# The causal mask of the first three units: from a VectorE product to a ScalarE copy and a GpSimd selection

## The chip, the cores and the metric

The kernel runs on one core of a Trainium2 chip. The core has five engines that work at the same time, each through its own queue in order: TensorE (matrix products and transposes, PE in the profile; PEld is its weight load), VectorE (DVE), ScalarE (ACT), GpSimd (POOL) and SyncE (SP), which here only issues transfers from the chip's main memory. TensorE writes its results to PSUM, a small memory of its own; the other tiles are in SBUF. The metric is the device time of one execution in microseconds, taken as the median of several runs.

## The reference

Two blocks follow one another. The first is a gated linear attention over 4 batches, 8 heads, 768 steps and a head size of 48. For each batch and head a 48x48 state decays by a gate and takes in one key and value at each step:

```python
f = 1.0 / (1.0 + np.exp(-f_logit))
for t in range(S):
    state = f[:, :, t, :, None] * state + np.einsum('bhd,bhe->bhde', k[:, :, t], v[:, :, t])
    y[:, :, t] = np.einsum('bhd,bhde->bhe', q[:, :, t], state)
```

The second mixes its output x, laid out as (4, 768, 384), along the sequence through a product of rank 32, and then along the channels through a hidden layer of 1536:

```python
u = x + h.transpose(0, 2, 1)          # h = x^T @ U @ V
out = u + np.maximum(u @ w_ch1, 0.0) @ w_ch2
```

All of it is float32.

## The kernel before

The sequence is cut into 12 chunks of 64 steps. Inside a chunk, each query meets the keys of its own and the earlier steps by a matrix product; between chunks the 48x48 states are carried by a scan. A **unit** is one batch and one pair of heads, so there are 16 units, `n = 0..15`, four to a batch (`HP = 4`). The two heads of a pair lie on two halves of the 128 partitions.

The work of a unit has a front and a rear. The front (`prepare`, line 643) has the pieces `gates` (transposes of the gates on TensorE, line 660, then a sigmoid on ScalarE, lines 681 and 682), `keep` (a backward scan of gate products on VectorE, L694, a small ScalarE copy `least`, L699, and three small VectorE operations, L701 to L704), `keys` (transposes of k, L660, and their product with that scan, L672), `read_back` (a forward scan, L712) and `queries` (transposes of q, L660, and their product with the forward scan, L672).

The rear (`attend`, line 770) has `kept` (transposes of k, L809, two ScalarE copies, `whole` L813 and `kb` L815), `states` (the chunk sums `ds`, L825, and a copy, L831), `scan` (the scan over chunks on VectorE, L846), `scores` (48 small products `sc`, L788, and the masked copy `A`, L795), `read` (products of the queries with the states, `y` L863, and a ScalarE copy of two columns, `seen` L870) and `inner` (products of `A` with the values added into the same `y`, L881, and the copy of `y` into `x`, L887).

A tile `A` is 128 x (2 heads, 6 blocks, 64 columns): 768 numbers for each partition. Partitions 0 to 63 hold one of a pair of chunks, 64 to 127 the other. In each 64x64 block the row is the key's step and the column the query's step, so an element counts where the column isn't smaller than the row. `causal` (lines 574 to 579) is a 128x64 tile of ones, zeroed elsewhere by two GpSimd selections of 64x64, and the mask is a product of the scores in PSUM with it.

The first batch has no channel mixing to stand beside it. Its four units run in a loop of their own (line 967), and the order of the pieces there is written out by hand for TensorE, VectorE and ScalarE; SyncE's and GpSimd's queues are ordered by the planner. In step `n` of that loop come:

```python
pieces = front(n, "keep", "keys") + rear(n - 1, "scan", "scores")
pieces += [lambda: busy(3)] + rear(n, "kept") + front(n, "read_back", "queries")
if n + 1 < HP:
    pieces += front(n + 1, "gates") + rear(n - 1, "read", "inner") + rear(n, "states")
```

So the scores of units 0, 1 and 2 are made in steps 1, 2 and 3 of this loop. The scores of unit 3 come just after it, and those of units 4 to 15 beside the mixing of the batch before. `busy(3)` is three matmuls into a tile that nobody reads (L962, tile `idle`).

The tiles in PSUM of the kind `ps_big` turn through three buffers: k's transposes, `sc`, `kept`'s transposes, q's transposes, the next unit's gates, `y` and `ds` take one after another. `A` has two buffers in SBUF. The rank-32 weights are put together from 64-bit words by ScalarE, VectorE and then a GpSimd sum, L95, beginning with `U` right after the loop.

A second path, `general_path`, stands behind a test on the gates and isn't run with these inputs.

Of the kernel before, what the change touches and what calls it, by code (L numbers as in the profile page):

```python
# [15 lines left out]
ALU = mybir.AluOpType  # L16
# [456 lines left out]
def factored_path(ctx, tc, q, k, v, f_logit, moe_U, moe_V, moe_w_ch1, moe_w_ch2, out, ok):  # L473
# [4 lines left out]
    nc = tc.nc  # L478
    B, H, S, D = q.shape
    P = nc.NUM_PARTITIONS  # L480
    C = P // 2
    NCH = S // C

    NBL = S // P
    HP = H // 2
# [90 lines left out]
    for s in range(2):  # L576
        half = causal[s * C : (s + 1) * C, :]
        nc.gpsimd.affine_select(out=half, in_=half, compare_op=ALU.is_ge, fill=0.0, base=0,
                                pattern=[[1, C]], channel_multiplier=-1)
# [190 lines left out]
    def attend(n):  # L770

        b, hp = divmod(n, HP)
        T = units[n]
# [4 lines left out]
        part = [slice(s * C, (s + 1) * C) for s in range(2)]  # L778

        def scores():  # L780


            T["A"] = two.tile([P, 2, NBL, C], F32, name="A")
            sc = ps_big.tile([P, 2, 512], F32, name="sc", tag="big")
            for c in range(NBL):
                for par in range(2):
                    for s in range(2):
                        nc.tensor.matmul(  # L788
                            sc[part[s ^ par], par, c * C : (c + 1) * C],
                            lhsT=T["k"][rows[par], chunk[2 * c + s]],  # L790
                            rhs=T["q"][rows[par], chunk[2 * c + s]],
                            start=True, stop=True,
                        )
            with tc.high_priority(offset=AHEAD):
                nc.vector.tensor_tensor(  # L795
                    T["A"],
                    sc[:, :, 0 : NBL * C].rearrange("p h (c i) -> p h c i", i=C),
                    causal.unsqueeze(1).unsqueeze(1).broadcast_to((P, 2, NBL, C)),
                    ALU.mult,
                )  # L800
# [71 lines left out]
        def inner():  # L872
# [18 lines left out]
            del units[n], v_tiles[n]  # L891

        return [kept, states, scan, scores, read, inner]

    ahead, here = {}, {}
# [59 lines left out]
    with tc.manual_schedule(engines={nc.vector.engine, nc.scalar.engine}):  # L955
# [62 lines left out]
        n = len(m.seconds) // (NBL // 2)  # L1018
# [386 lines left out]
```

## Time and profile before

| what | value |
| --- | --- |
| median of 5 runs | 489.61 us (489.17, 489.47, 489.61, 490.28, 494.36) |
| the profiled execution, its own time | 488.14 us |
| its span, from the first to the last instruction | 486.4 us |
| granted TensorE clock, mean | 0.995 |

Busy times of the first stretches (us):

| stretch | PE | DVE | ACT | POOL |
| --- | --- | --- | --- | --- |
| 0 to 14 | 10.68 | 7.17 | 4.65 | 4.68 |
| 14 to 24 | 8.83 | 9.50 | 4.04 | 0 |
| 24 to 33 | 8.74 | 8.20 | 4.01 | 0 |
| 33 to 40 | 6.86 | 5.80 | 2.86 | 0 |
| 40 to 47 | 4.63 | 5.77 | 3.54 | 1.84 |

A group in the profile is read as: line, engine, operation, the tile written, the tiles read, the shapes (partitions x elements), the count, then the busy time and the mean of one in nanoseconds, the idle time of the engine just before, and what ended it. In a timeline a row begins with the start and the duration in microseconds. The chain of waits goes back from the last instruction to what released each. The mask as a group, and GpSimd's selections in order of time:

```profile
L795 DVE TENSOR_TENSOR A<-sc,causal 128x768 f32<-128x768 f32 x16 | 15.2, 947 | 9.9 <-PE sc L788 9.9
```

```profile
2.21 0.23 POOL L578 TENSOR_SCALAR_AFFINE_SELECT causal<-causal 64x64 f32<-64x64 f32 x1
2.40 0.29 POOL masks.py:199 TENSOR_SCALAR_AFFINE_SELECT ident<-ident 128x128 f32<-128x128 f32 x1
2.76 0.24 POOL L578 TENSOR_SCALAR_AFFINE_SELECT causal<-causal 64x64 f32<-64x64 f32 x1
```

### The profile page before, as it was taken

How to read it: one execution, taken by the hardware profiler on the slowest of the kernel's cores; microseconds unless marked ns; L12 is line 12 of the kernel's file. 1: busy time of each engine (PE TensorE's matmuls, PEld its weight loads, DVE VectorE, ACT ScalarE, POOL GpSimd, SP SyncE). 2: the span in 40 equal slices, each digit the busy share in tenths (PEclk: the TensorE clock that was granted, in tenths of full speed). 3: DMA queues.
4: the chain of work that ended last, by engine and by line, in shares of the span. 5: the costliest groups of instructions: out<-in, count | busy, mean ns of one | idle time of the engine just before them, and what ended most of it. 6: DMA issues, size and time to landing. Idle time of an engine off the chain costs nothing.

```text
span 486.4 us, 12734 instructions
## 1 busy us (share of the span) xinstructions
PE 470.3 (97%) x5541; PEld 401.3 (82%) x5541; DVE 355.4 (73%) x563; ACT 163.3 (34%) x309; POOL 37.7 (8%) x49
## 2 busy tenths in 40 slices
PE   7997999999999999999999999999999999999995
PEld 4775788886566568899899888899979999999995
DVE  5888689777999757656857548797896886958642
ACT  2445566563334313424231403433231312112200
POOL 3002245453000000000000000000000000000000
PEclk9999899999999999999999999999999999999999
DMA  9979975666777512333536100100000000000001
GB/s 144 160 156 168 251 205 151 156 137 82 109 118 116 105 36 32 56 44 67 77 50 97 24 18 18 27 3 20 19 1 1 33 2 18 16 1 34 1 33 38
DMA packets 158679, 34.34 MB, mean 71 GB/s; under 512 B 149206, under 2 KB 157078, under 8 KB 158614
## 3 DMA queue, kind: packets, MB, share of 16 engines
q1 hardware_dynamic: 158614, 33.44, 37.3%
q8 instruction: 45, 0.74, 0.6%
q14 instruction: 20, 0.16, 0.1%
HBM read 28.70 MB, written 4.72 MB: 69 GB/s over the span
## 4 chain that ended last, share of the span: by engine, by line
PE 79%; DVE 9%; DMA 3%; issue 3%; SPq 2%; ACT 2%; DVEq 0%; ACTq 0%
PE pw L312 26%; PE pz L258 23%; PE pp L410 11%; PE y L863 2%; PE pt L660 2%; PE sc L788 2%; PE ds L825 2%; PE y L881 2%; DMA late<-in_f_logit_dram 2%; PE put L246 2%; PE po L283 2%; PE idle L962 2%; DVE late L712 1%; PE pt L809 1%; SPq L554 1%
## 5 line engine op out<-in xcount | busy, mean ns | idle before, releaser
L258 PE MATMUL pz<-uT,w 128*128 128x256 f32 x504 | 115.7, 383 | 0.0
L258 PEld LDWEIGHTS pz<-uT,w 128*128 128x128 f32 x504 | 93.4, 190 | 12.8
L312 PE MATMUL pw<-w,z_all 128*128 128x192 f32 x216 | 37.7, 329 | 0.0
L312 PE MATMUL pw<-zw,w_raw 128*128 128x192 f32 x216 | 37.4, 327 | 0.0
L312 PEld LDWEIGHTS pw<-zw,w_raw 128*128 128x128 f32 x216 | 35.2, 190 | 0.8 <-issue 0.6
L312 PEld LDWEIGHTS pw<-w,z_all 128*128 128x128 f32 x216 | 35.0, 190 | 0.7
L95 POOL TENSOR_TENSOR w<-w_y,w_r 128x384 int32<-128x384 int32 x24 | 31.5, 1313 | 41.7 <-DVE w_y L94 34.7
L694 DVE TENSOR_TENSOR_SCAN late<-fz,late 128x768 f32<-128x768 f32 x16 | 28.1, 1755 | 8.7 <-ACT fz L681 4.3
L268 ACT ACTIVATE z_all<-pz 128x512 f32<-128x512 f32 x33 | 19.7, 596 | 40.0 <-PE pz L258 39.9
L410 PE MATMUL pp<-v_nat,late 128*128 128x128 f32 x224 | 28.8, 275 | 0.0
L712 DVE TENSOR_TENSOR_SCAN late<-fz,other 128x768 f32<-128x768 f32 x16 | 27.9, 1745 | 0.1
L410 PEld LDWEIGHTS pp<-v_nat,late 128*128 128x128 f32 x224 | 27.0, 192 | 0.0
L283 PE MATMUL po<-w,zw 128*128 128x384 f32 x72 | 25.6, 499 | 0.0
L283 PE MATMUL po<-w,z_all 128*128 128x384 f32 x72 | 25.3, 496 | 0.3 <-DVE o L187 0.3
L403 ACT ACTIVATE other<-other 128x512 f32<-128x512 f32 x18 | 11.3, 631 | 39.9 <-DVE other L187 39.9
L851 ACT COPY st<-added 128x576 f32<-128x576 f32 x12 | 14.7, 1225 | 27.5 <-DVE added L846 27.5
L92 DVE TENSOR_SCALAR w_y<-w_y 128x384 f32<-128x384 f32 (+3 forms) x27 | 13.7, 507 | 13.9 <-ACT w_y L90 13.7
L795 DVE TENSOR_TENSOR A<-sc,causal 128x768 f32<-128x768 f32 x16 | 15.2, 947 | 9.9 <-PE sc L788 9.9
L283 PEld LDWEIGHTS po<-w,z_all 128*128 128x128 f32 x72 | 13.1, 190 | 8.7 <-DVE o L187 0.9
L283 PEld LDWEIGHTS po<-w,zw 128*128 128x128 f32 x72 | 12.9, 189 | 8.7 <-issue 1.2
L187 DVE TENSOR_TENSOR w_raw<-z_all 128x768 f32<-128x768 f32 x12 | 11.5, 955 | 10.6 <-ACT z_all L268 9.2
L312 PE MATMUL pw<-w,other 128*128 128x192 f32 x108 | 18.6, 327 | 0.0
(193 smaller groups left out, 827.4 us busy)
## 6 DMA issues: line engine op xcount, KB each, us to landing
w_raw<-in_moe_w_ch_dram SPq DMA_DIRECT2D x18, 384.0 KB, 3.7
out_dram<-o SPq DMA_DIRECT2D x24, 192.0 KB, 1.9
v_nat<-in_v_dram SPq DMA_DIRECT2D x16, 144.0 KB, 3.2
v_nat<-in_v_dram SPq DMA_DIRECT2D x32, 72.0 KB, 3.3
zw<-in_moe_w_ch_dram SPq DMA_DIRECT2D x6, 384.0 KB, 6.0
late<-in_f_logit_dram SPq DMA_DIRECT2D x10, 96.0 KB, 3.1
late<-in_k_dram SPq DMA_DIRECT2D x10, 96.0 KB, 2.8
late<-in_q_dram SPq DMA_DIRECT2D x10, 96.0 KB, 2.6
```

Of the source, the lines that this page charges most:

```text
L92: nc.vector.tensor_scalar(f, f, SMALLEST, LARGEST, ALU.max, ALU.min)
L95: nc.gpsimd.tensor_tensor(dst.bitcast(I32), shaped(y.bitcast(I32)), shaped(r), ALU.add)
L187: nc.vector.tensor_tensor(*args)
L258: nc.tensor.matmul(pm[:, i * 2 * P : (i + 1) * 2 * P], lhsT=w1[:, m, o : o + P], rhs=uT[a][:, m, :], start=(m == 0), stop=(m == NDC - 1))
L268: nc.scalar.activation(z[a, c][:, k : k + 2, :].rearrange("p i t -> p (i t)"), pm, AF.Relu)
L283: nc.tensor.matmul(pm, lhsT=z[a, i // NI][:, i % NI, s * P : (s + 1) * P], rhs=w2[:, i, :], start=(i == 0), stop=(i == NFC - 1))
L312: nc.tensor.matmul(pm[:, n * HM : (n + 1) * HM], lhsT=lhs[:, i, :], rhs=rhs[:, i, :], start=(i == 0), stop=(i == NI - 1))
L410: nc.tensor.matmul(pm[:, i, r * P : (r + 1) * P], lhsT=room["w"](wn)[:, r * P : (r + 1) * P], rhs=x_node(a, xn), start=((xn, wn) == of[0]) ...
L694: nc.vector.tensor_tensor_scan(backwards(X, S - 1, S), backwards(f, S, S), backwards(ends, S - 1, S), 0.0, ALU.mult, ALU.add,)
L712: nc.vector.tensor_tensor_scan(Y, f[:, 0:S], starts, 0.0, ALU.mult, ALU.add)
L795: nc.vector.tensor_tensor(T["A"], sc[:, :, 0 : NBL * C].rearrange("p h (c i) -> p h c i", i=C), causal.unsqueeze(1).unsqueeze(1).broadcast ...
L851: nc.scalar.copy(st, states.rearrange(by_e, c=NCH))
```

## The change

For units 0, 1 and 2 (`n < HP - 1`), `scores` no longer multiplies by `causal` on VectorE. ScalarE copies the scores from PSUM into `A`, and GpSimd then goes over `A` in place, once for each half of the partitions, and writes zero where the column is smaller than the row. The other thirteen units keep the product. The matrix products are the same.

```diff
@@ -791,6 +791,14 @@
                             rhs=T["q"][rows[par], chunk[2 * c + s]],
                             start=True, stop=True,
                         )
+            if n < HP - 1:
+
+                nc.scalar.copy(T["A"].rearrange("p h c i -> p h (c i)"), sc[:, :, 0 : NBL * C])
+                for s in part:
+                    half = T["A"][s].rearrange("p h c i -> p (h c) i")
+                    nc.gpsimd.affine_select(out=half, in_=half, compare_op=ALU.is_ge, fill=0.0, base=0,
+                                            pattern=[[0, 2 * NBL], [1, C]], channel_multiplier=-1)
+                return
             with tc.high_priority(offset=AHEAD):
                 nc.vector.tensor_tensor(
                     T["A"],
```

## The prediction

> **What bounds the kernel now.** I read the busy shares first, then the chain of work that ended last, cut to the stretch in which the first four units run, then that stretch in order of time.
>
> From the page:
>
> ```profile
> PE 470.3 (97%) x5541; PEld 401.3 (82%) x5541; DVE 355.4 (73%) x563; ACT 163.3 (34%) x309; POOL 37.7 (8%) x49
> PE 79%; DVE 9%; DMA 3%; issue 3%; SPq 2%; ACT 2%; DVEq 0%; ACTq 0%
> ```
>
> TensorE is busy for 97% of the span and carries 79% of the chain. The change touches about 15 to 42 us alone, so what counts is that stretch's own limit. The chain of waits there (start, us, what):
>
> ```profile
> 14.65 5.44 DMA late<-in_f_logit_dram
> ...
> 23.41 0.70 PE ds L825 x48
> 24.11 0.81 PE pt L660 x6
> 24.91 0.90 PE sc L788 x45
> 25.82 2.13 PE idle L962 x6
> 27.95 0.52 PE pt L809 x12
> 28.47 1.46 PE pt L660 x12
> 29.93 1.19 PE y L863 x44
> 31.11 0.02 issue
> 31.14 0.17 ACT seen L870
> ```
>
> Up to 20.09 the chain waits for unit 2's gates to land. From there to 37.29 it is TensorE's own queue, with one stop a unit for the small ScalarE copy "seen". VectorE isn't on it. One round, from k transposes to k transposes, is 32.89 - 24.04 = 8.85 us, and 2.13 us of it are filler matmuls (L962). So VectorE is nearly full (9.50 of 10 us busy from 14 to 24, 8.20 of 9 from 24 to 33) and still isn't the limit: it waits 0.55 us for the k transposes at 24.95 and 0.76 at 33.81.
>
> The operations to be exchanged, and what stands beside them, from the timeline (start, duration):
>
> ```profile
> 25.83 1.35 DVE L846 TENSOR_TENSOR_SCAN st<-added,whole 128x576 f32<-128x576 f32 x1
> 27.09 0.93 DVE L795 TENSOR_TENSOR A<-sc,causal 128x768 f32<-128x768 f32 x1
> 27.21 0.67 ACT L813 COPY whole<-whole 128x576 f32<-128x576 f32 x1 [2.23 <-DVE st L846]
> 27.94 1.75 DVE L712 TENSOR_TENSOR_SCAN late<-fz,other 128x768 f32<-128x768 f32 x1
> 31.35 0.92 PE L881 MATMUL y<-v_nat,A 64*64 64x48 f32 x48 [0.26 <-ACT seen L870]
> ```
>
> The reader is to see the distance between the end of the mask (28.02) and its first reader L881 (31.35): 3.3 us of room. For unit 0 the mask ends at 19.52 and L881 starts at 22.50; for unit 2, 36.88 and 41.92.
>
> [...]
>
> ```profile
> 72.23 1.75 DVE L694 TENSOR_TENSOR_SCAN late<-fz,late 128x768 f32<-128x768 f32 x1
> 72.45 2.31 POOL L95 TENSOR_TENSOR w<-w_y,w_r 128x384 int32<-128x384 int32 x1 [1.38 <-DVE w_y L94]
> 74.01 0.79 DVE L701 TENSOR_SCALAR X<-late 128x12 f32<-128x12 f32 x1
> ```
>
> L95 takes 1.00 us undisturbed. Here it was issued into a scan, ended 0.78 after it, and L701 (0.17 alone) stood until 74.80. [...]about 0.2 us of its start lies under the wait. An L95 beside L672, which reads PSUM and one SBUF tensor, was undisturbed (94.91, 1.00 us).
>
> [...]
>
> **The change, part by part.** Only units 0, 1 and 2 take the new branch.
>
> Removed: three VectorE products, each 0.93 us long and 0.85 in cadence (27.09 to 27.94): 2.6 us of VectorE work.
>
> Added on ScalarE: three PSUM copies of 128x768. The like row is L815, 0.80 us. They stand behind "least" (L699) and ahead of "whole" (L813), where ScalarE is idle for 2.23 to 2.47 us: scores end near 15.9, 25.8 and 34.6, so the copies run about 16.3-17.1, 25.9-26.7, 34.7-35.5, done before L813 can start (18.76, 27.21, 36.06). L815 and the sigmoid queue behind L813 and keep their times. Cost nothing; without that idle time it would be 0.8 us each.
>
> Added on GpSimd: six selections of 64x768. The trace has 64x64 at 0.23-0.24 us and 128x128 at 0.29: 0.055 us for 64 more elements, so 0.235 + 704 x 0.00086 = 0.84. [...]From above, L95's slope ((1.00 - 0.45)/256 = 2.15 ns an element) gives 1.00 + 384 x 0.00215 = 1.83. I take s = 0.9 and keep 0.8 to 1.8. GpSimd has nothing else between 5.4 and 42.29 (U, L95).
>
> [...]Both scans, L846 and L712, have two SBUF inputs; L672 has one. A blocked selection needs s - 0.2 = 0.7 after release; a blocked scan saves about 0.14.
> - Unit 0: copy to 17.1; selection one 17.2-18.1 holds off L846, which ends 19.3 (18.67 before); selection two to 20.0; L712 to 21.6 (21.19); q product to 22.65 (22.25); the next L694 starts 0.45 late. The k product would be ready at 24.40 + 0.45 = 24.85, but TensorE's transposes end at 24.92: nothing is lost. A is there at 20.0, wanted at 22.50.
> - Unit 1: selection one waits for L846 (27.18), ends 27.9; L712 to 29.5 (29.69); selection two to 30.2, wanted at 31.35; q product to 30.55 (30.75). L694 still waits for the sigmoid (30.76).
> - Unit 2: L846 ends 36.03, selection one 36.7, L712 38.35 (38.54), q product 39.4 (39.60), selection two 39.05, wanted at 41.92.
>
> So VectorE gets back little of the 2.6 us: selection one sits where the mask sat. On TensorE's path nothing moves, but that unit 3's scores (39.73), which need that q product, could start up to 0.2 earlier. PSUM: the scores' buffer comes free at 17.1 instead of 19.5, but its next user, the f transposes, has its data at 20.09 only. The "ds" tile at 23.23 takes the buffer that the q product frees: 22.65 leaves 0.5 us. That is the thinnest cover.
>
> No DMA is added or moved in the text; SP's queue could be ordered otherwise by the planner, at a price that I bound by the smallest and largest steps between its issues there, some 2 us either way. The cover of the six selections is the room ahead of L881 and the 2.13 us of filler on TensorE; without it each unit would pay 2s + 0.8 - 0.93, some 1.7 us.
>
> Sum: 0 to -0.2 us, I take -0.1: 488.14 - 0.1 = 488.0 for an execution like the profiled one (span 486.4 and 1.7 around it). The median, 489.61, lies 1.5 above that execution: 489.5.
>
> **The rivals.**
> 1. Slower: GpSimd's selection is dear. In the first round the q product ends, without the hidden parts, at 17.2 + 2s + 1.35 + 1.75 + 0.95, so "ds" (23.1) waits from s = 0.93 on, 2 us for each us of s. At s = 1.83 that is 1.8; in the second round selection two ends at 34.6 while L881 would start at 33.1: 1.5; in the third the q product is 0.9 late. Sum 4.2 us: 493.8. It passes 1% (4.9 us) near s = 2.1. For it: L95's slope. Against it: the 64x64 and 128x128 rows. Chance 0.06, and 0.12 that s is 1.0 to 1.6, costing 0.3 to 3 us.
> 2. VectorE's queue did set the round, its idle time being an artefact of the order. Then 3 x 0.85 = 2.6 us come off: 487.0. For it: 9.50 busy of 10 us. Against it: the chain, and the contention above. Chance 0.07.
> 3. The planner orders SP's transfers otherwise, and the wait for gates (5.44 us) or the weights after 46 us move: 487.6 to 491.6. The queue is nearly full there (DMA share 1.20 from 14 to 24). Chance 0.05.
>
> **How the numbers follow.** Hidden, 0.70: 489.5. The range takes in the repeats around the median (489.17 to 490.28 but for one) and reaches down into rival 2's upper part and up through most of the half-dear selection: 488.5 to 491.8. About 1% is what a measurement of this kernel can tell from no change. Faster by that much: 0.02, since even rival 2 gives 0.5%; slower 0.07, rival 1's upper end with something of 3; within 0.91.
>
> **What would show it.** Right: L881 still released by "seen" (22.5, 31.35), filler and transposes of unit 2 within 0.3 us of their times, six selections of 0.8-1.0 us, up to 2.7[...], L846 of unit 0 about 2.0 us long. Wrong: L881 released by POOL, "ds" by a late q product, or a round shorter than 8.85 us.

## The result and the profile after

The changed kernel takes 491.38 us in the median of 42 runs, the kernel before 489.06 us in 79. The ratio is 1.0052, 95% interval 1.0038 to 1.0066: a small loss, some 2.5 us by the ratio, where no change was forecast. The profiled execution took 491.84 us (span 490.1).

The exchange itself went nearly as worked out. From the timeline of the changed kernel (start, duration, engine and line; the matmul rows are L889 for `inner` and L871 for `read`, eight lines further down than before):

```profile
15.51 0.80 ACT L796 COPY A<-sc 128x768 f32<-128x768 f32 x1 [0.21 <-PE sc L788]
16.33 1.35 DVE L854 TENSOR_TENSOR_SCAN st<-added,whole 128x576 f32<-128x576 f32 x1
16.38 4.29 POOL L799 TENSOR_SCALAR_AFFINE_SELECT A<-A 64x768 f32<-64x768 f32 x2 [10.94 <-ACT A L796]
17.59 2.38 DVE L712 TENSOR_TENSOR_SCAN late<-fz,other 128x768 f32<-128x768 f32 x1
20.08 0.96 DVE L672 TENSOR_TENSOR qT<-pt,late 128x768 f32<-128x768 f32 x1
22.50 1.53 PE L889 MATMUL y<-v_nat,A 64*64 64x48 f32 x48 [0.35 <-ACT seen L878]
```

The reader is to see how the two engines hold each other up. The first selection (16.38 to 18.37) lasts 1.99 us and ends 0.69 us behind the scan L854, L712 beside it takes 2.38 us where it takes 1.75 alone, and the second selection (from 18.43) lasts 2.24 us and ends 0.70 us behind L712; a selection alone took 0.90 (c3, c8). `A` is complete at 20.67 and is read at 22.50, released by `seen` and not by GpSimd. Up to 48 us no product on TensorE is released by a late operation of VectorE or GpSimd.

Where the time went is seen in the chain of waits (start, us, what), of the changed kernel:

```profile
22.50 1.53 PE y L889 x48
24.03 1.28 PE ds L833 x48
...
36.05 0.84 PE idle L970 x2
36.89 1.59 issue
38.48 1.56 PE idle L970 x4
...
43.71 0.43 issue
...
46.60 2.01 issue
48.60 0.28 PE y L871
```

and of the kernel before:

```profile
22.50 0.91 PE y L881 x48
23.41 0.70 PE ds L825 x48
...
40.41 0.98 issue
41.40 0.73 PE sc L788 x31
...
44.20 1.38 issue
```

"issue" is time in which TensorE waited for nothing that the profile shows: 1.59 + 0.43 + 2.01 = 4.03 us after, 0.98 + 1.38 = 2.36 before. And at 22.50 the same 48 products take 1.53 us in place of 0.91. The windows say why; after the busy time and count of the five engines, the columns are the granted clock, the DMA share and GB/s. The changed kernel:

```profile
22.00:26.00 4.00, 3.65 (x105) 3.44 (x102) 2.04 (x4) 1.38 (x4) 0.00 (x0) 0.57 0.72 121
```

The kernel before:

```profile
22.00:26.00 4.00, 3.74 (x159) 3.26 (x154) 3.38 (x7) 1.55 (x4) 0.00 (x0) 1.00 0.65 114
```

The clock stood at half for 3.41 us there, from 22.21; a second such stretch, near 50 us, is in both profiles (from 49.52 after, 51.73 before). When the channel mixing begins, the changed kernel is 3.7 us late (first L258 at 59.03, 55.31 before), and that is the whole difference of the two spans. The two groups of products from 22.50 on make 1.2 of it (2.81 us in place of 1.61), the issue gaps 1.7.

One execution proves little, since the clock differs from run to run. Over its runs the mean granted clock is 0.9928 in the changed kernel, and 0.994 to 0.997 in the five groups of runs of the kernel before that stood beside the experiments. Among runs with a clock of at least 0.998 the changed kernel takes 489.5 us on the mean (8 runs) and the kernel before, in those five groups, 487.7 (76 runs). So some 1.8 us of the 2.5 are there without any loss of clock, and the rest goes with the clock.

What else is new in TensorE's queue is seen in what its lines hold besides matmuls. EVENT_SEMAPHORE stands there as an instruction of its own, 51 ns long, and is read here as a wait (count, min/median/max ns); the changed kernel, from 10 to 56 us:

```profile
L871 PEldq EVENT_SEMAPHORE  x4: 51/51/51, 20.2 to 45.2; - x4
L889 PEldq EVENT_SEMAPHORE  x3: 51/51/51, 22.4 to 44.5; - x3
```

The kernel before has one of them, at `read`, and none at `inner`: six instructions more. They come from the change. The f transposes take the scores' PSUM buffer, and their weight loads used to be released by VectorE's mask; now the view names ScalarE and no VectorE operation (before, then after):

```profile
20.20 0.64 PEld L660 LDWEIGHTS pt<-ident,late 128*128 128x128 f32 x6 [1.12 <-DVE A L795]
20.11 0.64 PEld L660 LDWEIGHTS pt<-ident,late 128*128 128x128 f32 x6 [1.45 <-ACT kb L823]
```

In the kernel before, VectorE's scan for `read` ran ahead of the mask (unit 1: 25.83 and 27.09), so a wait for the mask covered the scan too. Without it each unit's `read` needs a wait for VectorE of its own and each `inner` one for GpSimd. This is read from the order of the program; the counts of the experiments fit it (c2, without the selections: three more at `read`, none at `inner`; c4 and c8, with the product and GpSimd behind it: three more at `inner`, none at `read`).

### The profile page after: what moved, and what is told of

Its sections match the earlier page's. It is cut to its first block, busy times and chain, and to the rows that moved or that the text cites. A ratio compares the mean times of both kernels' runs of the same rounds, so it can differ in the third digit from the quotient of the medians.

```text
span 490.1 us, 12748 instructions
## 1 busy us (share of the span) xinstructions
PE 470.9 (96%) x5541; PEld 401.7 (82%) x5541; DVE 355.4 (73%) x560; ACT 165.8 (34%) x312; POOL 48.7 (10%) x55
## 4 chain that ended last, share of the span: by engine, by line
PE 78%; DVE 10%; DMA 3%; issue 3%; SPq 3%; ACT 2%; DVEq 0%; ACTq 0%
PE pw L312 26%; PE pz L258 23%; PE pp L410 11%; PE y L889 2%; PE y L871 2%; PE sc L788 2%; PE ds L833 2%; PE pt L660 2%; DMA late<-in_f_logit_dram 2%; PE po L283 2%; PE put L246 1%; SPq L548 1%; DVE late L712 1%; DVE late L694 1%; PE pt L817 1%
## 5 line engine op out<-in xcount | busy, mean ns | idle before, releaser
L258 PE MATMUL pz<-uT,w 128*128 128x256 f32 x504 | 115.7, 383 | 0.3 <-ACT uT L247 0.3
L258 PEld LDWEIGHTS pz<-uT,w 128*128 128x128 f32 x504 | 93.4, 190 | 13.3 <-issue 0.5
L95 POOL TENSOR_TENSOR w<-w_y,w_r 128x384 int32<-128x384 int32 x24 | 31.5, 1313 | 40.4 <-DVE w_y L94 32.5
L694 DVE TENSOR_TENSOR_SCAN late<-fz,late 128x768 f32<-128x768 f32 x16 | 28.1, 1756 | 9.5 <-ACT fz L681 4.8
L712 DVE TENSOR_TENSOR_SCAN late<-fz,other 128x768 f32<-128x768 f32 x16 | 29.8, 1864 | 0.1
L889 PEld LDWEIGHTS y<-v_nat,A 64*64 64x64 f32 x768 | 14.1, 145 | 7.1 <-issue 3.8
L803 DVE TENSOR_TENSOR A<-sc,causal 128x768 f32<-128x768 f32 x13 | 12.4, 950 | 9.9 <-PE sc L788 9.9
L871 PEld LDWEIGHTS y<-st,qT 48*64 48x64 f32 x704 | 13.7, 138 | 6.9 <-issue 6.4
```

What stands on the lines that cost most here:

```text
L95: nc.gpsimd.tensor_tensor(dst.bitcast(I32), shaped(y.bitcast(I32)), shaped(r), ALU.add)
L258: nc.tensor.matmul(pm[:, i * 2 * P : (i + 1) * 2 * P], lhsT=w1[:, m, o : o + P], rhs=uT[a][:, m, :], start=(m == 0), stop=(m == NDC - 1))
L694: nc.vector.tensor_tensor_scan(backwards(X, S - 1, S), backwards(f, S, S), backwards(ends, S - 1, S), 0.0, ALU.mult, ALU.add,)
L712: nc.vector.tensor_tensor_scan(Y, f[:, 0:S], starts, 0.0, ALU.mult, ALU.add)
L871: nc.tensor.matmul(o(c % 2, par, c // 2), lhsT=T["q"][rows[par], chunk[c]], rhs=T["st"][rows[par], c, :], start=(c <= 2), stop=False, skip ...
L889: nc.tensor.matmul(o(s, par, c), lhsT=T["A"][part[s ^ par], par, c, :], rhs=vt[part[s ^ par], c, par, :], start=False, stop=True, skip_gro ...
```

## The experiments

Every kernel was timed beside the kernel before. The theories are P (VectorE's scans and GpSimd's selections hold each other up), C (the clock falls by chance of timing), Q (TensorE's new waits; Q1 by their number, Q2 only where GpSimd is late), S (only where in TensorE's stream the issue gaps fall counts) and H (ScalarE's queue held behind `seen`).

### Four parts of the change

c1_again is the changed kernel. c2_copy_only leaves out the selections, so that `A` of units 0 to 2 stays unmasked (against the changed kernel):

```diff
                 nc.scalar.copy(T["A"].rearrange("p h c i -> p h (c i)"), sc[:, :, 0 : NBL * C])
-                for s in part:
...
                 return
```

c3_beside keeps the product, with copy and selections on memory that `z_all` uses only later:

```diff
+            if n < HP - 1:
+                twin = z_all[:, 0:3, :].rearrange("p i t -> p (i t)").rearrange("p (h c i) -> p h c i", h=2, i=C)
+                nc.scalar.copy(twin.rearrange("p h c i -> p h (c i)"), sc[:, :, 0 : NBL * C])
+                for s in part:
+                    half = twin[s].rearrange("p h c i -> p (h c) i")
...
             with tc.high_priority(offset=AHEAD):
```

c4_pool_wait keeps the product and selects one block after it:

```diff
+            if n < HP - 1:
+                for s in part:
+                    half = T["A"][s, 0, NBL - 1, :]
+                    nc.gpsimd.affine_select(out=half, in_=half, compare_op=ALU.is_ge, fill=0.0, base=0,
+                                            pattern=[[1, C]], channel_multiplier=-1)
```

> The changed kernel once more, for a second profile. Theory Q (TensorE's queue: the products that read A and the state each have one more wait on another engine's semaphore[...]): the issue gaps of TensorE between 35 and 50 us add up to about 4 us again, against 2.4 us before; ratio 1.004 to 1.006. Theory C (the granted clock falls to half once more in the first 30 us by chance of timing): ratio near 1.005 only where the trace shows such a stretch at 22 to 26 us; without it 1.000 to 1.002. Theory P[...]: ratio 1.005, and a product on TensorE that is released by a late VectorE or GpSimd operation.

> The changed kernel without the six selections: A of units 0 to 2 stays unmasked, the part above the diagonal isn't zeroed. VectorE is relieved of three products, [...]nobody waits for GpSimd; only the wait on VectorE ahead of the products with the state is left of the new waits. Theory P: as before or faster, 0.994 to 1.000. Theory Q: about half of the loss stays, 1.001 to 1.004. Theory C: 1.000 to 1.005, by what the clock does.

> The kernel before, with its products by the mask, and beside them the three copies and six selections on a tile that nobody reads. TensorE has the waits of before. Theory P: slower by as much as the changed kernel or more, 1.005 to 1.012. Theory Q: 1.000 to 1.001. Theory C: 1.000, unless the clock drops at 22 to 26 us in its trace too.

> The kernel before, and after each product by the mask two small selections (64x64) on one block of A, which change nothing in it but make TensorE's products with A wait for GpSimd too. Half of the new waits, hardly any work. Theory Q: 1.001 to 1.004. Theory P: 1.000. Theory C: 1.000, unless the clock drops.

Measured: 1.0061 (1.0040 to 1.0082), 0.9996 (0.9981 to 1.0011), 0.9993 (0.9979 to 1.0007), 1.0019 (1.0003 to 1.0034). P falls: with copies, selections and the old products all running (c3), nothing is lost. VectorE's relief with three new waits at `read` (c2) gains nothing that can be told from zero, and three waits for GpSimd (c4) cost less than the whole change. c1's TensorE rows (idle time and releaser at the end):

```profile
26.25 0.68 PE L788 MATMUL sc<-qT,kz 48*64 48x64 f32 x27 [0.88 <-issue]
42.54 0.74 PE L788 MATMUL sc<-qT,kz 48*64 48x64 f32 x34 [0.70 <-issue]
47.01 0.28 PE L871 MATMUL y<-st,qT 48*64 48x48 f32 x1 [2.00 <-issue]
```

Here the clock is full at 22 to 26 us and the loss is there all the same, so C isn't the cause alone. The gaps are 3.58 us, the last one again ahead of the last product of `read`.

### Waits, lateness and place

c5_small_select is the changed kernel with the selections of c4, so that all blocks of `A` but one stay unmasked in units 0 to 2. c6_shift is the kernel before with two tiny matmuls, and c7_after_shift the changed kernel with them:

```diff
-            pieces += [lambda: busy(3)] + rear(n, "kept") + front(n, "read_back", "queries")
+            pieces += [lambda n=n: (busy(3), tiny(1 if 1 <= n < 3 else 0))] + rear(n, "kept") + front(n, "read_back", "queries")
```

where `tiny` is a matmul of 16 columns into `idle`, four instructions. c8_select_too is the kernel before with the change's six selections after its products.

> The changed kernel with both selections of a unit cut to 64x64, one block of A: all other blocks of units 0 to 2 stay unmasked. TensorE's waits are exactly those of the changed kernel, GpSimd's work is small and its result is there some 4 us before TensorE asks. Theory Q1 (the number of waits alone: six more instructions in TensorE's queue and its stops there): 1.004 to 1.007. Theory Q2 (the waits matter only where GpSimd's result is late[...]): 0.999 to 1.002.

> The kernel before with one more tiny filler matmul (16 columns) in each of the second and third rounds: no wait is added, but TensorE's stream is 8 instructions longer ahead of 40 us[...]. Theory S[...]: a change of 0.3% or more in either direction, with issue gaps elsewhere. Theories Q1 and Q2: 0.999 to 1.001.

> The changed kernel with the same two tiny filler matmuls. Theory S: the loss changes by 0.3% or more, to 1.003 or under or 1.009 or over. Theories Q1 and Q2: 1.005 to 1.007, as without them.

> The kernel before, with its products by the mask, and then the six full selections over A, which change nothing in it but come later than in the changed kernel. TensorE waits for GpSimd ahead of the products with A; the wait on VectorE ahead of the products with the state isn't added. VectorE isn't relieved. Theory Q2: 1.004 to 1.008. Theory Q1: 1.001 to 1.003, as with the small selections (1.0019). Theory S: 1.001 to 1.003.

Measured: 1.0086 (1.0048 to 1.0125), 1.0028 (1.0010 to 1.0045), 1.0031 (1.0006 to 1.0056), 1.0027 (1.0007 to 1.0046). Q2 falls with c5: GpSimd has hardly anything to do, and the whole loss is there. Its TensorE rows:

```profile
41.57 0.74 PE L788 MATMUL sc<-qT,kz 48*64 48x64 f32 x34 [0.98 <-issue]
46.31 0.28 PE L871 MATMUL y<-st,qT 48*64 48x48 f32 x1 [2.27 <-issue]
```

In c8, too, GpSimd was late once (`inner` at 31.57 was released by it), and 1.0027 is under Q2's 1.004. But c6 has no new wait and loses too, which Q1 doesn't give, and c7 has all six and loses no more than c6, against Q1's 1.005 to 1.007. So the place seemed to count.

### Place against waits

c9_fewer and c10_before_fewer have the filler of the second and third rounds as matmuls of 512 and 512 columns, eight instructions fewer; c11_regrouped has 512, 512 and 128:

```diff
+        def wide(*cols):
+            for c in cols:
+                nc.tensor.matmul(idle[:, 0:c], lhsT=ident, rhs=ends[:, 0:c], start=True, stop=True)
...
-            pieces += [lambda: busy(3)] + rear(n, "kept") + front(n, "read_back", "queries")
+            pieces += [lambda n=n: wide(512, 512) if 1 <= n < 3 else busy(3)] + rear(n, "kept") + front(n, "read_back", "queries")
```

> The changed kernel with the filler of the second and third rounds as two matmuls of 512 columns in place of three of 384: 8 instructions fewer in TensorE's stream, which makes up for the six that the new waits add, and 128 columns (0.24 us) a round less. All new waits stay. Theory S[...]: 0.998 to 1.002, and the large issue gap near 45 us lies in L208 again, behind the last product with the state. Theory Q1[...]: 1.004 to 1.008.

> The kernel before with the same filler of two matmuls of 512 columns. Theory S: [...]0.997 to 1.001. Theory Q1: 0.998 to 1.000, the 0.24 us a round.

> The changed kernel with that filler as matmuls of 512, 512 and 128 columns: as many instructions and as many columns as in the changed kernel, so a check on the regrouping alone. Theory S: 1.004 to 1.008, the gap ahead of the last product with the state as in the changed kernel. Theory Q1: the same.

Measured: 1.0023 (1.0005 to 1.0041), 1.0006 (0.9985 to 1.0027), 1.0060 (1.0034 to 1.0087). c9's gap did move into L208, but a loss stays, in neither theory's range. Then c12 and c13 moved ScalarE's conversions ahead of `seen` (in the changed kernel and in the one before), and c14 added one tiny matmul, four instructions, to the kernel before:

```diff
-        pieces += loads[1:2] + rear(n - 1, "inner") + rear(n, "read") + loads[2 : early + 1]
+        pieces += loads[1:2] + rear(n - 1, "inner") + loads[2 : early + 1] + rear(n, "read")
```

> The kernel before with one tiny filler matmul (16 columns, four instructions on TensorE) in the second round; no wait, no operation of another engine is changed. Theory S: [...]1.003 to 1.006, the gap ahead of the last one of them. Theory Q1: 1.000 to 1.001.

> The changed kernel, with the pieces that put together V and the first block of the hidden layer's weights placed ahead of the products with the state of unit 3. TensorE's queue is the same; ScalarE's copy seen, which waits for those products, no longer stands ahead of four conversions. Theory H (the gap costs so much because ScalarE's queue is held behind seen[...]): 1.001 to 1.004. Otherwise (the length of the gap and the clock alone): 1.005 to 1.007 as with the changed kernel.

> The kernel before with the same pieces moved, as a check on the move alone. Theory H: 0.998 to 1.001, since seen isn't held there. Otherwise 0.999 to 1.002.

Measured: c14 0.9999 (0.9983 to 1.0015), c12 1.0053 (1.0030 to 1.0076), c13 1.0007 (0.9987 to 1.0026). H falls. c14, to which S gave 1.003 to 1.006 with the gap ahead of the last product of `read`, lost nothing; but its gap stands ahead of the first L208 product:

```profile
46.33 1.16 PE L208 MATMUL ph<-x,U 128*32 128x288 f32 x12 [2.64 <-DVE w_y L93]
```

The view puts it down to VectorE, but the weights that this product reads, `U`, were ready at 43.13. So c15_six added exactly six instructions, with no wait, to the kernel before, and c16_four_fewer took four out of the changed kernel (the filler of 512 and 512 in the second round alone):

```diff
+        def tiny():
+            nc.tensor.matmul(idle[:, 0:16], lhsT=ident, rhs=ends[:, 0:16], start=True, stop=True)
+            nc.tensor.transpose(idle[:, 0:P], ident, ident)
...
+            pieces += [lambda n=n: (busy(3), tiny() if n == 1 else None)] + rear(n, "kept") + front(n, "read_back", "queries")
```

> The kernel before with six instructions more on TensorE in the second round (a filler matmul of 16 columns and a transpose of 128x128, some 0.15 us together), as many as the changed kernel's new waits add; no wait and no other engine is changed. Theory S: the gap lies ahead of the last product with the state of unit 3, as in the changed kernel, and the ratio is 1.003 to 1.006. Theory Q1: 1.000 to 1.001.

> The changed kernel with the filler of the second round alone as two matmuls of 512 columns: four instructions fewer, so that two more than before are left, and 0.24 us less filler. All new waits stay. Theory S: the gap lies ahead of or inside the first L208 product, and the ratio is 1.000 to 1.002. Theory Q1: 1.004 to 1.007.

Measured: c15 1.0019 (1.0002 to 1.0036), c16 1.0048 (1.0026 to 1.0069). c15 lies in neither theory's range, c16 in Q1's (1.004 to 1.007) and not in S's (1.000 to 1.002). So S falls as the main cause. The gap of c15 stands where the changed kernel's does:

```profile
45.67 0.28 PE L863 MATMUL y<-st,qT 48*64 48x48 f32 x1 [1.69 <-issue]
```

and goes with a loss of 0.2% in place of 0.5%; that of c16 stands ahead of L208, where nothing was lost in c14, and the loss stays, with gaps in the rounds before it:

```profile
26.50 0.58 PE L788 MATMUL sc<-qT,kz 48*64 48x64 f32 x25 [0.87 <-issue]
38.98 0.91 PE L970 MATMUL idle<-late,ident 128*128 128x384 f32 x2 [1.49 <-issue]
48.09 2.05 PE L208 MATMUL ph<-x,U 128*32 128x288 f32 x12 [1.92 <-ACT w_y L90]
```

All kernels together, by the instructions added to TensorE's stream (tiny matmuls, filler taken out and waits) and the new waits among them:

| added | no new wait | three waits | all six |
| --- | --- | --- | --- |
| -8 or -2 | 1.0006 (c10) | | 1.0023 (c9) |
| 0 | 0.9993 (c3), 1.0007 (c13) | | |
| 2 to 4 | 0.9999 (c14) | 0.9996 (c2), 1.0019 (c4), 1.0027 (c8) | 1.0048 (c16) |
| 6 | 1.0019 (c15) | | 1.0052 (changed kernel), 1.0061 (c1), 1.0086 (c5), 1.0060 (c11), 1.0053 (c12) |
| 8 or 14 | 1.0028 (c6) | | 1.0031 (c7) |

Down a column is the place, along a row the waits. At about the same place the kernels with six waits lose 0.5% more (c16 against c14) and 0.3% more (changed kernel against c15); these intervals don't overlap. In the last row they lose no more (c7 against c6). The means of the columns are 1.0009, 1.0014 and 1.0052; place alone moves a ratio by up to 0.3%. Every kernel in the last column is the changed kernel, with VectorE's products gone and GpSimd ahead of `inner`: c2, c3 and c5 show that VectorE's relief, the delays between scans and selections and GpSimd's time, each by itself, aren't what costs; but six waits on the kernel before were not tried.

## Why the prediction was wrong

**The number.** 491.38 us lies inside the range that was stated in microseconds, but by luck: the kernel before took 489.06 beside it and not 489.61. Against its own kernel before the change lost some 2.5 us, where 0 to 0.2 of gain was worked out.

**The bound** was right: TensorE's queue sets this stretch, and VectorE's three products were worth nothing there. c2 (0.9996) has three new waits that could hide a small gain, but its round without the products takes 9.04 us, no less than the 8.85 of before. Rival 2, a gain of 2.6 us, didn't come. Rival 3 didn't either: SyncE's transfers start in the same order, unit 2's gates are waited for 5.36 us (5.44 before), and from there to 62 us no transfer is on the chain.

**ScalarE's copies at nothing** were right: 0.80 us each, in idle time, shown by c2.

**The price of the selection** was right. An undisturbed one took 0.896 us in c3 and 0.899 in c8, where 0.9 was taken; rival 1 (1.0 and more) didn't come. Beside a scan a selection lasted up to 2.24 us in the changed kernel, within the 2.7 allowed.

**Scans and selections** held each other up as the scan L694 and the sum L95 had in the profile before (L95 2.31 us, alone 1.00): L712, with two SBUF inputs, lasted 2.38 us beside a selection in place of 1.75. The order in unit 0 differed, since the copy ended at 16.31 and not 17.1 and the selection came behind L854 rather than ahead of it, which so took 1.35 us and not 2.0; the q product, at 20.08, was no later than before (21.29). In c3 all of this costs nothing (0.9993).

**"On TensorE's path nothing moves"** is the step that failed. The prediction priced each new wait by whether its data would be there in time, and they were. It left the six waits themselves out of its sum: that a wait stands in the queue of the engine that sets the end, and that a wait removed with the mask had covered others. In its place the runs show a loss of 0.52% on the mean of the eight kernels with all six waits, and of 0.1% in the ten others (the kernel before counted as one of them, with none): 2.1 us more.

Where these 2.1 us lie is known only roughly. Directly, `inner` starts 0.35 us after the last product of `read` where it was 0.26, in two of the three units: 0.2 us. The rest is indirect. Over one profile each, the eight kernels have gaps of 3.8 us from 13 to 60 us on the mean (2.7 to 5.6), the ten others 2.9 (2.4 to 3.5): 0.9 us. Counted with the issue gaps are the stops ahead of L208 in c4, c14 and c16 that the view puts down to another engine. And the mean granted clock over all runs is 0.9931 in the eight, against 0.9949 in the others: 0.18% of the span, 0.9 us of full clock, of which a lost us goes with some 0.7 us of time in the runs of before: 0.6 us. Together that is 1.7 of the 2.1 us; the remainder isn't placed.

**The clock** wasn't priced at all. In the profiles of the kernel before and of the changed one the half-clock stretches inside the first 60 us last 3.41 us, and the two of the changed kernel start 27.31 us apart. In c10 and c12 TensorE's products are slow for longer, from 22.6 on (in c10 four groups from 22.60 to 28.38 take 1.53, 1.50, 1.54 and 1.56 us, and their like from 34.02 on 0.91, 0.88, 0.87 and 0.93). What starts such a stretch was not shown. In the changed kernel a gap of 2.01 us, ended at 48.60, went ahead of the one from 49.52. But such a gap doesn't decide it: c3 and c13 both have one of 1.94 us near 45 us, and only in c13 the eleven L208 products behind it are slow (2.13 us, in c3 1.16). Between 45 and 55 us seven of the eight kernels with all six waits have slow products in their profiles (the 48 of `inner` take 1.27 to 1.53 us, in c9 0.92), and three of the ten others (the kernel before, c10 and c13). The stretch from 22.21 isn't the change's own: in c10, with no new wait, the same 48 products take 1.53 us at 22.60 as well.

What stays open is how a wait makes the gaps. The profiles of the kernel before and of the changed one have 45 packets of 16,384 bytes each on an instruction queue, and the five issue gaps summed above end 2.3 to 2.9 us after one of these packets starts. In the kernel before, the packet at 42.68 us starts 1.5 us before the gap (44.20), in the changed kernel that at 46.2 only 0.4 us before (46.60). Whether packets, waits and gaps hang together was not shown, and no run measured what TensorE does at such a wait beyond its 51 ns. Nor was the change tried without its waits: `A` has to be complete before it is read.

## What to carry to other kernels

Before moving work off an engine that isn't the bound, list what the bounding engine will wait for afterwards: a wait that goes away may have covered later ones, and those then stand in its queue as instructions of their own, here six of 51 ns each. Data that was there in time didn't make up for it here: the kernels with the six waits lost 0.5% on the mean. And when an edit changes the number of instructions, compare it with a neutral edit of the same length before a loss of a few tenths of a percent is put down to the edit's meaning.

## What the runs showed of the hardware

- Six instructions more on TensorE without any new wait (c15), or eight (c6), went with a loss of 0.2% (interval 0.02% to 0.36%) and 0.3% (0.10% to 0.45%) in a kernel of 12,734 instructions, while with four (c14) no loss was seen.
- A GpSimd selection over 64x768 floats takes 0.896 us alone. It and a scan with two SBUF inputs held each other up: in the changed kernel a scan beside it took 0.63 us more (2.38 for 1.75) and a selection up to 1.3 more (2.24 for 0.90). This left no trace in the total (c3: 0.9993).
- Single executions of the kernel before ranged from 486.65 to 494.66 us over 79 runs. In the five groups with a clock for each run, a granted clock lower by 0.01 went with some 3.2 us more.
- In the changed kernel's profile the granted clock was at half for 3.41 us from 22.21 and again from 49.52. Of two kernels with the same gap of 1.94 us in TensorE's queue, c3 and c13, one had slow products behind it (eleven in 2.13 us) and one had not (1.16).
